# One eight-bank PSUM tile in place of four two-bank tiles, and another hand-written order, in a fused H3 and MLP block

## The chip, the cores and the metric

The kernel runs on one core of one Trainium2 chip. The metric is the device time of one execution in microseconds (us); less is better. TensorE (PE) multiplies matrices into PSUM, ScalarE (ACT) and VectorE (DVE) read PSUM and work in SBUF, GpSimd (POOL) does small set-up work and issues some DMAs, and SyncE (SP) issues the other DMAs.

## The reference

For a sequence of 2048 rows of 640 channels (`q`, in bfloat16) the block computes

```python
xn = layernorm(q)                                  # no scale, no shift
k_shift = sum_t pad(k)[:, t:t+S] * shift_k[:, 3-t] # 4 taps
kv = k_shift * v
y  = irfft(rfft(pad(kv)) * rfft(pad(ssm_k)))[:S]   # causal convolution, length 2048, per channel
s  = xn * (y + kv * ssm_D)
h  = gelu(xn @ w1 + b1)                            # 640 -> 1728, tanh form
g  = silu(h @ w2 + b2)                             # 1728 -> 640
out = q + s * g
```

Two independent paths meet only in the last line: the convolution (K for the filter, U for `kv`) and the two-layer MLP.

## The kernel before, in words

The 2048 rows are 16 tiles of 128 partitions by 640 channels. The convolution is a Fourier transform done in matrix products with two exchanges through scratch memory in HBM. In stage 1 (`stage1`), TensorE multiplies each of the 16 tiles of the filter (tokens `K1_i`) and of `kv` (`U1_i`) with a table `W`; ScalarE or VectorE evicts the pair of PSUM banks to a staging buffer (`Ke_i`, `Ue_i`). The last 128 channels of four tiles go together (`K1r_Q`, `Ker_Q`, `U1r_Q`, `Uer_Q`). Each group Q of four tiles is written to scratch by one DMA of 1280 KB (`Ks_Q`, `Us_Q`); the staging buffer `st` has room for two groups, so a group's first eviction waits until the group two before it has landed. In stage 2, eight slices s are loaded back (`KL_s`, `UL_s`), transformed (`K2`, `U2`, `X2`; evictions `Kf`, `Uf`), multiplied on VectorE (`pr`, `pq`) and transformed back (`i1`, `i1r`; evictions `ie`, `ir`). The results go to scratch (`cs_s`), come back (`cl_r`), and a last product (`i2_i`) gives the convolution, which VectorE multiplies with xn (`ym_i`).

`kv` itself is VectorE's: for each of five groups r of rows (four tiles each in 0 to 2, two each in 3 and 4) a chain of eight steps, `kvr_0`, `kvr_1m`, `kvr_1a` to `kvr_3a`, `kvr_4` (L502 to L511). They read `k` (loads `kl`), the taps (`skl`) and, in the last step, `v` (`vl`).

The MLP works on chunks c of four tiles. `bn_i`, `rs`, `xn_i` make the layer norm; `xt_i`/`xe_i` (TensorE and an eviction) or a transposing DMA (`xT_c`, chunks 2 and 3) turn it. The first layer is `f1_c_r_ft`: five matmuls (L423) into one PSUM bank for 128 of the 1728 hidden channels and 512 rows (256 for the first five of chunk 0), and a gelu on ScalarE (`ge`, L427) that reads the bank. `f1h`/`geh` do the last 64 channels. With `/N` a group is issued as two halves of 64 columns each. The second layer is `f2_i_h`: 14 matmuls (L463) for a tile and half of the channels, a silu (`si_i`, L470), the product with xn (`gx_i`, L473), and at the end the sum with x (`ad_i`) and the store (`os_i`).

Nothing decides at run time or by rule. `plan.op` lists every operation with its engine, what it reads and writes, and which pooled buffers it takes; the string `ORDER` names all operations in the order in which they are recorded, so it is the program order of every engine and of every DMA queue. In a token such as `K1_15@2.0`, the numbers after @ are the places of the buffers that it takes first, here PSUM banks 2 and 3 and staging place 0; `/A`, `/D`, `/G`, `/S` choose ACT, DVE, POOL or SP. The PSUM pool `ps` has eight places, one for each bank of 2 KB in a partition. An operation takes a pair (an even place and the next) or one bank. `emit` (L78) checks that a place is free when it is taken, and sets no semaphore. Those come from the layer below, which follows reads and writes of each declared tile and makes an instruction wait for earlier ones on other engines. In this kernel the eight banks are four tiles of two banks; a pair is a whole tile, and a single is one half of it:

```python
ps_t = [psum.tile([P, 2, 512], F32, name="ps%d" % i)[:] for i in range(4)]        # L155
ps = Pool(8, lambda k, sz: ps_t[k // 2] if sz == 2 else ps_t[k // 2][:, k % 2, :]) # L177
```

Every eviction of `evict` (L175) is one instruction, whatever it evicts; the profile tells them apart by tile (`st`, `k`, `v`, `lat`, `xnT`, `G`). The engines work through their instructions in order, so an instruction that waits holds all behind it.

## Time and profile before

| | |
|---|---|
| median of 3 runs | 226.44 us (223.7 to 226.59) |
| the profiled execution's time | 223.6 us |
| its span (first to last instruction) | 221.8 us |
| TensorE busy | 179.5 us, 81% |
| VectorE busy | 154.7 us, 70% |
| ScalarE busy | 137.9 us, 62% |
| GpSimd busy | 26.5 us, 12% |
| moved by DMA | 51.98 MB, 234 GB/s over the span |
| granted TensorE clock, mean | 0.985 |
| Ks_0 issued, landed | 74.46, 79.89 us |
| Us_3 issued, landed | 100.66, 106.18 us |
| last inverse transform (i1_5) ended | 178.47 us |

The profile is of one execution. Times of instructions are from the start of its span. A line of the list of waits says which engine and line waited for which, for how long in all, how often, and the longest. A line of a timeline gives start, length, engine, source line, operation, what it writes and reads, and in brackets the idle time ahead of it and what ended it. In the chain that ended last, pieces stand in order of time (start, length, what). A token's time is found by counting an engine's instructions in the order of `ORDER`.

### The profile page before, as it was taken

What the parts mean: (1) busy time and instruction counts of PE and PEld (TensorE: products, weight loads), DVE (VectorE), ACT (ScalarE), POOL (GpSimd) and SP (SyncE); (2) the same over time, 40 slices, a digit from 0 to 9 for tenths busy, and PEclk for the clock granted to TensorE, in tenths of its full rate; (3) what the DMA queues carried; (4) which work ended last, traced back from release to release, by engine and by line L of the source; (5) the groups of instructions that cost most, each with busy time, mean ns of one, the idle gap of its engine ahead of it and who ended that gap; (6) DMA issues with size and microseconds to landing.
All of it is one profiled execution on the core that took longest, in us unless ns stands there. A gap on an engine that the chain in (4) does not pass through costs nothing.

```text
span 221.8 us, 5581 instructions
## 1 busy us (share of the span) xinstructions
PE 179.5 (81%) x2405; PEld 105.2 (47%) x2406; DVE 154.7 (70%) x241; ACT 137.9 (62%) x192; POOL 26.5 (12%) x59
## 2 busy tenths in 40 slices
PE   7965795655868998869778978978997799996893
PEld 2434443333323565536455434534443366685792
DVE  7986999999993004669578686877885621786852
ACT  6986696648274986469775868879697672111011
POOL 4831030000000041001500010200200103000000
PEclk9999999999788999999999999999999999999999
DMA  7999957579550499977989942880643356992154
GB/s 202 384 427 417 409 205 259 218 249 415 223 236 3 177 314 336 404 308 240 296 296 192 168 123 92 226 280 5 205 156 118 121 202 206 415 342 114 42 200 148
DMA packets 22299, 51.98 MB, mean 234 GB/s; under 512 B 6657, under 2 KB 15746, under 8 KB 20866
## 3 DMA queue, kind: packets, MB, share of 16 engines
q1 hardware_dynamic: 19968, 41.78, 53.8%
q0 software_dynamic: 2160, 9.83, 12.8%
q8 instruction: 19, 0.31, 0.6%
q14 instruction: 6, 0.05, 0.1%
q10 hardware_dynamic: 146, 0.00, 0.0%
HBM read 31.95 MB, written 18.35 MB: 227 GB/s over the span
## 4 chain that ended last, share of the span: by engine, by line
PE 40%; ACT 27%; DMA 24%; issue 5%; DVE 3%; SPq 1%; ACTq 0%; DVEq 0%
PE ps L423 21%; PE ps L463 10%; ACT st L175 10%; ACT hT L427 8%; DMA scrU<-st 7%; DMA v<-scrC 5%; DMA lat<-scrU 4%; DMA xnT<-xn 4%; PE ps L587 3%; ACT k L175 2%; DMA xn<-in_ssm_k 2%; ACT v L175 2%; DMA scrC<-k 2%; PE ps L544 1%; ACT sl L470 1%
## 5 line engine op out<-in xcount | busy, mean ns | idle before, releaser
L423 PE MATMUL ps<-xnT,w 128*128 128x512 bf16 (+2 forms) x340 | 65.6, 374 | 23.0 <-ACT hT L427 16.6
L463 PE MATMUL ps<-w,hT 128*128 128x320 bf16 (+2 forms) x602 | 64.5, 299 | 3.7 <-ACT st L175 1.3
L463 PEld LDWEIGHTS <-hT 128*128 128x128 bf16 (+2 forms) x602 | 47.4, 104 | 19.4 <-issue 7.1
L423 PEld LDWEIGHTS <-w 128*128 128x128 bf16 (+1 forms) x340 | 29.2, 103 | 54.7 <-issue 36.1
L427 ACT ACTIVATE hT<-ps,b1f 128x512 bf16<-128x512 f32 (+1 forms) x57 | 36.3, 656 | 27.0 <-PE ps L423 26.6
L175 ACT CAST st<-ps 128x1024 bf16<-128x1024 f32 x39 | 37.6, 1021 | 8.4 <-PE ps L338 4.3
L470 ACT ACTIVATE sl<-ps 128x640 bf16<-128x640 f32 (+1 forms) x17 | 11.5, 677 | 32.2 <-PE ps L463 32.1
L473 DVE TENSOR_TENSOR xn<-xn,sl 128x640 bf16<-128x640 bf16 (+1 forms) x17 | 7.9, 465 | 32.2 <-ACT sl L470 32.2
L175 ACT CAST k<-ps 128x1024 bf16<-128x1024 f32 (+2 forms) x22 | 17.9, 855 | 3.5 <-PE ps L544 1.6
L509 DVE TENSOR_TENSOR lat<-lat 128x2560 bf16<-128x2560 bf16 (+1 forms) x15 | 19.4, 1296 | 0.5
L506 DVE TENSOR_TENSOR lat<-k,lat 128x2560 bf16<-128x2560 bf16 (+1 forms) x15 | 18.3, 1222 | 0.3
L175 ACT CAST v<-ps 128x1024 bf16<-128x1024 f32 (+2 forms) x18 | 14.4, 830 | 3.7 <-PE ps L587 1.8
L647 DVE TENSOR_TENSOR xn<-ps,xn 128x640 bf16<-128x640 f32 x16 | 12.7, 818 | 3.7 <-PE ps L643 3.7
L175 DVE CAST k<-ps 128x1024 bf16<-128x1024 f32 (+2 forms) x11 | 9.4, 858 | 8.0 <-PE ps L544 3.6
L370 DVE BATCH_NORM_STATS2 stats<-x 128x6 f32<-128x320 bf16 x32 | 13.6, 468 | 0.2 <-DMA x<-in_x 0.2
L175 DVE CAST lat<-ps 128x1024 bf16<-128x1024 f32 (+2 forms) x9 | 9.1, 1013 | 6.5 <-PE ps L544 2.2
L175 DVE CAST v<-ps 128x1024 bf16<-128x1024 f32 (+2 forms) x8 | 7.6, 955 | 4.6 <-PE ps L587 2.1
L175 ACT CAST lat<-ps 128x1024 bf16<-128x1024 f32 (+2 forms) x12 | 8.2, 728 | 2.6 <-PE ps L544 1.3
L544 PEld LDWEIGHTS <-F 64*32 64x32 bf16 x512 | 5.8, 91 | 8.0 <-issue 4.0
L321 PE MATMUL ps<-hT 128*128 128x512 bf16 x23 | 7.8, 489 | 1.3 <-DVE hT L206 1.2
L587 PE MATMUL ps<-st,I 32*64 32x512 bf16 x256 | 8.3, 379 | 0.0
L528 POOL DMA_DIRECT2D k<-scrK x3 | 2.6, 853 | 47.3 <-DMA scrK<-st 47.1
(98 smaller groups left out, 178.0 us busy)
## 6 DMA issues: line engine op xcount, KB each, us to landing
scrK<-st SPq DMA_DIRECT2D x4, 1280.0 KB, 5.4
scrU<-st SPq DMA_DIRECT2D x4, 1280.0 KB, 6.4
v<-in_v SPq DMA_DIRECT2D x4, 640.0 KB, 12.6
out<-x SPq DMA_DIRECT2D x15, 160.0 KB, 2.5
w<-in_w SPq DMA_DIRECT2D x2, 1120.0 KB, 9.4
x<-in_x SPq DMA_DIRECT2D x3, 640.0 KB, 6.4
k<-in_k SPq DMA_DIRECT2D x3, 640.0 KB, 8.0
k<-scrK POOLq DMA_DIRECT2D x3, 640.0 KB, 5.5
```

Source lines behind the costliest of these rows:

```text
L175: (nc.scalar.copy if e == "ACT" else nc.vector.tensor_copy)(out=out_, in_=in_)
L370: nc.vector.bn_stats(out=stats[:, i, h, :], in_=x_t[:, i, h * H:(h + 1) * H])
L423: nc.tensor.matmul(out=pb.v[us, 0:b - a], lhsT=w1_t[:, ft, t, us], rhs=xnTb[c].v[:, a // P:b // P, t, :], start=(t == 0), stop=(t == DT - 1))
L427: nc.scalar.activation(out=hTb[c].v[:, ft, a:b], in_=pb.v[:, 0:b - a], func=ACT.Gelu_apprx_tanh, bias=b1_f[:, ft:ft + 1], scale=1.0)
L463: nc.tensor.matmul(out=pb.v[us, h, 0:H], lhsT=hTb[c].v[0:M, ft, q * P + us.start:q * P + us.stop], rhs=w2_t[0:M, ft, hs], start=(ft == 0), ...
L470: op("si_" + nm, "ACT", lambda e, hs=hs, n=n: nc.scalar.activation(out=s_.v[:, hs].rearrange("p (h c) -> p h c", c=H), in_=pb.v[:, n[0]:n[ ...
L473: op("gx_" + nm, "DVE", lambda e, hs=hs: nc.vector.tensor_tensor(out=xn_t[:, i, hs], in0=xn_t[:, i, hs], in1=s_.v[:, hs], op=ALU.mult), re ...
L506: op("kv%d_%dm" % (r, j), "DVE", lambda e, i=i, n=n, j=j, t=t, wb=wb: nc.vector.tensor_tensor(out=t.v[:, 0:n, :], in0=k_t[:, i + 3 - j:i + ...
L509: op("kv%d_%da" % (r, j), "DVE", lambda e, n=n, t=t, a=a: nc.vector.tensor_tensor(out=a.v[:, 0:n, :], in0=a.v[:, 0:n, :], in1=t.v[:, 0:n, ...
L544: nc.tensor.matmul(out=pb.v[32 * j:32 * j + 32, a, ri * wd:(ri + 1) * wd], lhsT=F2_t[64 * a:64 * a + 64, ri, :], rhs=B.v[64 * a:64 * a + 6 ...
L587: nc.tensor.matmul(out=pb[j // 2].v[64 * a:64 * a + 64, j % 2, :], lhsT=I1_t[32 * j:32 * j + 32, m, :], rhs=o[w][32 * j:32 * j + 32, a, r, ...
L647: op("ym_%d" % i, "DVE", lambda e, i=i, pb=pb: nc.vector.tensor_tensor(out=xn_t[:, i, :], in0=pb.v.rearrange("p a b -> p (a b)")[:, 0:D], ...
```

## The change

The eight banks are declared as one tile; pairs and singles are views of it at the same places. All the rest of the code is the same. `ORDER` is another permutation of the same 693 operations, with other places for the buffers and in places another engine for an eviction or a queue for a DMA.

```diff
-    ps_t = [psum.tile([P, 2, 512], F32, name="ps%d" % i)[:] for i in range(4)]
+    ps_t = psum.tile([P, 8, 512], F32, name="ps")[:]
...
-    ps = Pool(8, lambda k, sz: ps_t[k // 2] if sz == 2 else ps_t[k // 2][:, k % 2, :])
+    ps = Pool(8, lambda k, sz: ps_t[:, k:k + 2, :] if sz == 2 else ps_t[:, k, :])
...
 ORDER = """
-zz wu0@0 grid fix Dl sm0 c0 wu2@1 b1l wq2 Kl4 wq1 ws2 K1_15@2.0 K1_13@4 sm1 id wq0 sm2 wu5@6 ws1 xl0 bn0 rs0 xl1 bn1
...
-kv1_0@1 kv1_1a kv1_2m@0 kv1_2a kv1_3m@0 kv1_3a kv1_4 Ks_1 U1_1@0.2 kl2 Ue_1/A K1_9@4 Ke_9/A kv2_0@0 kv2_1m@1 kv2_1a
-f1h_0@2 geh_0 kl3 f1_1_0_5/N@3 f1_0_0_10/N@6 ge_0_0_10 f1_0_0_9/N@7 ge_1_0_5 one1 ge_0_0_9 f1_1_0_2/N@0 ge_1_0_2 Ks_2
-U1r_0@4 Uer_0/A U1_0@2 Ue_0/A U1_2@6 kv2_2m@1 kv2_2a kv2_3m@1 kv2_3a Ue_2/A w2l0 vl2 kv2_4 kv3_1m@1 f1_0_1_0@1
-ge_0_1_0 f1_1_0_11@0 ge_1_0_11 kv3_0@0 kv3_1a f1_1_0_8@4 ge_1_0_8 f1_0_0_8@5 ge_0_0_8 vl3 w2l1 U1_3@2 Ue_3/A K1_3@6.0
-Ke_3/A K1_2@0 Ke_2/A f1_1_0_3@4 ge_1_0_3 Da kv3_2m@1 kv3_2a Us_0 f1_1_0_9@5 ge_1_0_9 f1_0_0_12@2 ge_0_0_12 f1_1_0_4@3
-kv3_3m@1 ge_1_0_4 K1r_0@6 K1_0@0 Ker_0/A Ke_0/A one0 kv3_3a kv3_4 K1_1@4 f1_1_0_10@2 f1_0_0_11@3 Ke_1/A Ks_0 KL2/G@0
-xl4 ge_1_0_10 ge_0_0_11 U1_5@6.2 Ue_5/A U1_6@0 Ue_6/A xl5 f2_7_0@4.0 f2_7_1 si_7 U1_4@2 Ue_4/A kv4_0@1 U1r_1@6
-U1_10@0.0 Ue_10/A f2_2_1@4.1 Uer_1/A f2_2_0 U1_7@2 Ue_7/A U1r_2@0 Uer_2/A si_2 U1_9@6 Ue_9/A kv4_1m@0 kv4_1a gx_2
...
+grid zz wu3@0 fix c0 Kl4 wq2 b1l sm0 Dl wu2@1 ws2 wq1 ws1 one1 K1_12@2.0 xl1 Ke_12/A K1_14@4 Ke_14/A K1_13@6 Ke_13/A
...
+kv2_1a Ke_8/A Ks_2 f1_0_0_5@2 kv2_2m@0 kv2_2a kv2_3m@0 ge_0_0_5 f1_0_0_7@3 ge_0_0_7 U1_2@6.2 U1_3@4 Ue_3/A U1_0@0
...
+U1r_0@0 Uer_0/A U1_1@6 Ue_1/A Us_0 f1_1_0_7@2 ge_1_0_7 ge_0_1_0 f1_1_0_9@3 ge_1_0_9 f1_0_0_10@4 ge_0_0_10 K1_2@0.0 kl3
+kv3_0@0 K1_1@6 K1_3@2 kv3_1m@1 kv3_1a Ke_3/A f1_0_0_9@5 Ke_2/A ge_0_0_9 kv3_2m@1 f1_0_0_11@4 ge_0_0_11 kv3_2a Ke_1/A
+Da f1_0_1_4@2 ge_0_1_4 f1_1_0_11@3 ge_1_0_11 K1r_0@0 Ker_0/A K1_0@4 kv3_3m@1 Ke_0/A U1_4@6.2 Ue_4/A f1_0_1_1@2 kv3_3a
+ge_0_1_1 xl5 f2_7_1@0.0 f2_7_0 si_7 U1_5@4 U1_7@6 Ks_0 U1r_1@2 f2_2_1@0.1 Uer_1/A Ue_7/A xl4 vl3 gx_7 kv3_4 Ue_5/A
+U1_6@2 Ue_6/A Us_1 U1r_2@6.0 f2_2_0 U1_11@4 Uer_2/A kv4_0@1 kv4_1m@0 kv4_1a U1_9@2 Ue_11/A si_2 kv4_2m@0 kv4_2a U1_8@6
+Ue_8/A Ue_9/A f2_5_1@4.0 kv4_3m@0 kv4_3a f2_5_0 U1_12@0.2 kv4_4 si_5 gx_5 U1_13@6 Ue_13/A U1_10@2 KL1@0 KL2@1 Ue_12/A
...
+Uf_0_1/A UL2@8 f2_0_0@4.0 U2_2_1@0 Uf_2_1/A pr_1_0@0 X2_1@2 Kf_1_2/A pr_1_1@1 pr_0_0@2 Uf_1_2/A KL4/G@9 K2_4_0@6
...
+Uf_2_2/D ge_3_0_3 pq_1_0@0 i1_0@0.2 pq_0_0 ie_0_0/A xT2@0 pq_0_1 U2_2_0@6 Uf_2_0/D f1_2_0_10@4.0 ge_2_0_10 f1_2_0_1@5
+ie_0_1/D f1_2_0_7@0 ge_2_0_1 UL3@10 ge_2_0_7 pq_1_1 i1r_0@6.2 ir_1_1/A ir_0_0/A ir_1_0/A ir_0_1/A pr_2_1@1 f1_3_0_9@1
...
```

## The prediction, before the changed kernel ran

> **What bounds the kernel now.** I read the page first, then the list of waits, then the timelines of TensorE and ScalarE around the longest waits, then the chain that ended last. "Before TensorE's matmul" below means the idle time ahead of it. The page:

> ```profile
> PE 179.5 (81%) x2405; PEld 105.2 (47%) x2406; DVE 154.7 (70%) x241; ACT 137.9 (62%) x192; POOL 26.5 (12%) x59
> PE   7965795655868998869778978978997799996893
> PEclk9999999999788999999999999999999999999999
> ```

> TensorE is the busiest engine, and its busy row dips to 5 and 6 in slices 3 to 11 (about 11 to 66 us), where no other row is idle for long. From slice 12 on it is mostly at 8 or 9. So about 42 us of TensorE's span is idle, most of it early. The list of waits says for whom (total, times, longest):

> ```profile
> PE ps L423 <- ACT hT L427: 16.6, 15, 2.4
> ...
> PE ps L423 <- ACT hT L443: 5.5, 3, 2.8
> ```

> 22 of the 42 us are one kind: a first-layer matmul (L423) that waits for a gelu. It doesn't need the gelu's result. It waits for a PSUM bank. Which bank is seen around the longest, the matmul at 45.89 (token f1_1_0_5/N@3, bank 3):

> ```profile
> 42.33 0.74 PE L437 MATMUL ps<-xnT,w 128*64 128x256 bf16 x10
> 45.89 2.35 PE L423 MATMUL ps<-xnT,w 128*64 128x512 bf16 x20 [2.83 <-ACT hT L443]
> ...
> 41.59 0.69 ACT L427 ACTIVATE hT<-ps,b1f 128x512 bf16<-128x512 f32 x1 [1.36 <-PE ps L423]
> 42.18 2.83 ACT L175 CAST st<-ps 128x1024 bf16<-128x1024 f32 x3
> 44.88 0.96 ACT L443 ACTIVATE hT<-ps,b1f 64x256 bf16<-64x256 f32 x2
> ```

> Bank 3 was last read by ge_1_0_1, the gelu at 41.59, free at 42.28. The matmul started at 45.89, when geh_0 (44.88 to 45.84) had read bank 2, the other half of the same two-bank tile. The wait list of the built program says the same: it waits for the tile, not for the bank. With one eight-bank tile and the old order, 77 of TensorE's waits move to an earlier instruction in that list, and a matmul into one bank waits for that bank's own reader only; in the new program I find no wait for a neighbour's bank.

> **Part 1, the tile.** For each of these waits I took from the timelines the start of the matmul, the end of TensorE's work before it, and the end of the reader that it really needs. What would be saved on the spot: 0.7 before xt0, 1.8 before f1_0_0_0, 0.5, 0.6, 0.7, 1.3, 1.3, 0.7, 2.8 (f1_1_0_5), 0.7, 2.4 (f1_1_0_11, at 55.25), 0.7, 2.0 (f1_1_0_9, at 65.06), 0.7: 17.0 us up to 70 us. From 129 to 175 us seven more: 1.1, 0.8, 0.3, 0.7, 0.6, 1.2, 1.2: 5.9 us. Two of the early ones cost twice:

> ```profile
> 54.00:55.00 1.00, 0.00 (x0) 0.82 1.03 420
> 55.00:56.00 1.00, 0.75 (x2) 0.50 1.06 442
> 56.00:57.00 1.00, 1.00 (x4) 0.50 1.01 430
> ```

> (us, TensorE busy, granted clock, DMA share, GB/s.) After the idle 2.40 us before f1_1_0_11 the granted clock falls to 0.50, and again after the 2.08 us before f1_1_0_9. The ten matmuls after them took 3.69 and 3.90 us, where ten at full clock take 2.4: another 2.8 us. After the 2.83 us at 43 us the clock stayed at 1.00, so I count these two drops as gone with their gaps, and nothing more. [...] The trace has the drops right behind the gaps.

> **Part 2, the order.** It holds the same work: single-column or split (/N) first-layer groups both take about 1.2 us, so what moves is only what stands ahead of what. I added the incremental durations of the rows (first-layer group 1.19, second-layer half 1.96, ScalarE eviction of two banks 0.91, gelu 0.69, VectorE's kv steps 1.49 and, for the two half groups, 0.82) up to the store that ends each stage. ScalarE's total stays (132.1), VectorE's falls by 1.1. On POOL, 12% busy, two memsets and the scaling of the inverse table (sx) come earlier and hide; KL1 and KL2 go from POOL to SyncE, ahead of Us_2.

> (a) Up to the last store of the filter's first stage (Ks_0, issued at 74.46). TensorE has 47.9 us of work ahead of it before, 52.4 after: +4.5. Minus 17.0 and 2.8: 74.5 + 4.5 - 19.8 = 59.2. ScalarE has 51.7 us ahead of it, its first eviction starts at 5.7, and its first gelu brings 1.28 us that the sums leave out (in the chain at 16.16): 58.7 in all, so with TensorE at 59.2 it would have to run without a pause. Two in-order queues as full as that hold each other up: I give back 4 us, a fifth of the gain (bounds: 0 and all 19.8), and take 63.

> (b) Up to the landing of the last U store (Us_3, 106.18). The new SyncE order is Us_0, kl3, xl5, Ks_0, xl4, vl3, Us_1: two loads that used to go out by 46.84 now stand behind stores, and what is behind those waits too. kl3 is needed by kv3_0 and goes out with Us_0, which has 38.5 us of TensorE's work ahead of it, so near 48; it lands near 54 (1.9 MB at the rate below), and VectorE ended kv2 at 59.7. vl3 is needed by kv3_4. How fast transfers go in this stage:

> ```profile
> 74.50:80.00 5.50, 5.30 (x46) 3.51 (x45) 0.00 (x0) 5.47 (x7) 0.00 (x0) 1.00 0.87 300
> 80.00:106.20 26.20, 22.85 (x274) 14.59 (x272) 15.29 (x35) 17.71 (x21) 5.08 (x8) 1.00 0.89 322
> ```

> About 318 GB/s (last column). Ks_0, xl4 and vl3 are 2.6 MB, 8.2 us: vl3 lands at 71.2. kv3_4 and the eight steps of kv4, 9 x 0.82: 78.6. Last U matmuls (0.8) and two evictions (1.8): 81.2; a store alone takes 5.5 (Us_3 did): 86.7. But from Ks_0 to Us_3 the queues carry four stores of 1.31 MB (Ks_0, Us_1 to Us_3) and five loads of 0.66 (xl4, vl3, KL0 to KL2), 8.5 MB, 26.8 us at that rate: 89.8, and I take this later one: 16.4 us earlier than before. VectorE isn't in the way: before, kv4 stood behind gx_2 (68.6 to 86.4, idle); now it doesn't. [...] Us_1, with four POOL loads in flight, took 10.64 us and Us_3 5.53; if the queues were independent, the sum would be 202 instead.

> (c) To the last inverse transform (i1_5, ended 178.47) it was 72.3 us:

> ```profile
> 84.86 10.64 DMA scrU<-st
> ...
> 100.66 5.53 DMA scrU<-st
> ...
> 107.23 9.80 DMA lat<-scrU
> ...
> 208.39 9.73 PE ps L463 x140
> ```

> The chain goes from that landing through the U loads and then along TensorE. TensorE's work in it is 66.3 before, 66.6 after. Of the 5.9 us of bank waits I count 4 as gained: 89.8 + 72.3 + 0.3 - 4 = 158.4. UL3 now follows both transposes on SyncE; xT2 landed 9.4 us after issue, and TensorE has about 9 us of work between, so I charge nothing, and 2 us if that cover is gone.

> (d) To the end: 43.3 us before, nearly all TensorE; 0.7 us of its work now stands ahead of i1_5 instead. The last core stores (cs) and their reload took 10.4 us from i1_5 to i2_4, covered by 9.8 us of second-layer work; in the new order 11.1 us stand there. 158.4 + 42.6 = 201.0.

> The profiled execution had a span of 221.8 and a time of 223.6, 1.8 outside. 202.8 on that scale; the median of the runs (226.44) is 1.3% above that execution, so 205.5 as a time to be measured.

> **Rivals.** *Half comes back* (25%). ScalarE becomes the wait. For it: 58.7 against 59.2 in (a). Against it: ScalarE's gelus waited 26.6 us for L423 in the old order, so it was itself held by the bank waits. Half of 25.7: 223.6 - 12.9 = 210.7, as a median 213. *No change* (9%). The U path is set by VectorE's kv chain (9.8 of 10 us busy from 30 to 60) and by transfers, and TensorE's idle time only moves. Against: VectorE sat idle 17.8 us at 68.6, waiting for a silu behind TensorE. 224 to 228. *Slower: the stores hold ScalarE* (9%). Uer_2 now waits for Ks_0's landing (staging slot 0), Ue_13 for Us_1's, and behind each, gelus and evictions queue in order, and TensorE behind those when its banks are full. TensorE has 8 to 10 us of work between the last filter matmul and Uer_2; if the packed stores take Us_1's 10.64 instead of 5.4, it stalls. If ScalarE has also eaten all 19.8 of (a), Ks_0 goes at 79.0 and lands at 89.6, Us_1 near 100; from Us_1's landing to Us_3's it was 10.7 (95.5 to 106.2), so Us_3 lands at 111, 4.5 us later than before: 228, as a median 231. It decides once Ks_0 is issued after about 74. *The declaration doesn't free the banks*, or ties all eight: 1%; the wait lists speak against it; then 240 and more.

> **How the numbers follow.** The forecast (56%) is 197 to 210: 197 is without the 4 us of (a), the 2 of (c) and most of (b)'s transfer bound (3.1), 210 gives back 4.5 more. The half-back case reaches to 219. Faster by over 2% (about what a measurement of this kernel can tell from no change) is below 221.9: 56 + 25, 0.81; within 2% 0.09; slower 0.10. The range 197 to 220 leaves out the last three cases.

> **What would show it.** Right: the two waits of L423 for L427 and L443 together under 8 us; PEclk without dips after slice 2; Ks_0 issued at 60 to 66, Us_3 landed at 87 to 93, span 196 to 208. Wrong: ScalarE evictions waiting for scrK or scrU for over 5 us, kv3_4 idle for vl3 past 75 us, or TensorE's waits for hT unchanged.

## The result and the profile after

The changed kernel takes 192.05 us (median, 191.75 to 192.54) against 226.51 for the kernel before in the same comparison (223.7 to 227.97): a ratio of 0.852, with a 95% interval of 0.844 to 0.860. Here and below, a median is of all runs of a kernel, a ratio of those within 1.5% of its fastest. The forecast was 205.5, its range 197 to 220: the direction was right, the time lies below the range, and the gain was 34.5 us where 20.9 had been forecast. The profiled execution took 192.54 us, with a span of 190.8.

The page of the kernel after: busy time and instructions of each engine, then TensorE's busy tenths and the granted clock in 40 slices (4.8 us each).

```profile
PE 176.1 (92%) x2377; PEld 103.8 (54%) x2377; DVE 153.9 (81%) x241; ACT 138.7 (73%) x194; POOL 30.0 (16%) x61
PE   7889999999889874999979999999999999999991
PEclk9999999999999996699999999999999999999998
```

TensorE has the same products to make, and 14.7 us of idle time in place of 42. The dips to 5 and 6 in slices 3 to 12 are gone. One dip is new, in slices 15 and 16, and behind it the clock falls to half (0.50): from 73 to 80 us. The list of TensorE's waits says what stands there, and what no longer stands there:

```profile
PE ps L544 <- DMA k<-scrK: 3.6, 1, 3.6
PE ps L463 <- ACT st L175: 1.3, 2, 0.7
...
PE ps L544 <- DMA lat<-scrU: 0.8, 1, 0.8
```

The two lines of 16.6 and 5.5 us, L423 waiting for a gelu, have no counterpart. The longest wait is for a load. The chain that ended last follows it (start, length, what):

```profile
61.55 12.34 DMA k<-scrK
...
73.94 1.05 PE ps L544 x27
74.99 3.85 PE ps L463 x14
...
81.81 5.50 DMA scrU<-st
...
88.42 11.57 DMA lat<-scrU
```

From the issue of KL1 at 61.55 the chain goes through the load, K2_1_0 and K2_1_1 (L544), a second-layer half at half clock (14 matmuls in 3.85 us, which take 2.01 elsewhere) and the last U store to the U loads. Between 20 and 66 us three engines are nearly full at once, as one stretch of the windows of this kernel shows (busy us of PE, PEld, DVE, ACT, POOL, then clock, DMA share, GB/s):

```profile
20.00:66.00 46.00, 43.44 (x331) 23.20 (x330) 44.80 (x37) 43.76 (x63) 5.47 (x4) 1.00 0.99 375
```

Where the 31.0 us of span went, by three anchors: when Us_3 landed, when i1_5 ended, the end of the span; and TensorE's idle time in the two later stretches (length less busy time in the windows between the anchors). The other rows are the experiments below.

| kernel | Ks_0 issued | Us_3 landed | from there to i1_5 (TensorE idle) | from i1_5 to the end (idle) | span |
|---|---|---|---|---|---|
| before | 74.5 | 106.2 | 72.3 (10.8) | 43.3 (7.2) | 221.8 |
| after | 52.9 | 87.3 | 64.4 (1.7) | 39.1 (4.3) | 190.8 |
| tile_alone | 54.4 | 88.2 | 69.8 (8.1) | 42.7 (6.6) | 200.7 |
| order_alone | 73.9 | 105.9 | 77.9 (12.1) | 39.1 (4.3) | 222.9 |
| k2_late | 53.8 | 82.6 | 65.8 | 39.1 | 187.5 |
| new_tail | 55.2 | 90.4 | 69.6 | 39.7 | 199.7 |
| old_head | 57.1 | 90.8 | 64.9 (2.0) | 38.9 (4.4) | 194.5 |
| new_head | 52.9 | 86.0 | 66.8 (3.1) | 43.8 (7.7) | 196.6 |
| gap_filled | 52.4 | 83.2 | 64.7 | 38.6 | 186.6 |

So 18.9 us were gained before Us_3 landed, 7.9 between that and i1_5, 4.2 behind it.

### The profile page after: what moved, and what is told of

Its sections match the earlier page's. It is cut to its first block, busy times and chain, and to the rows that moved or that the text cites. A ratio compares the mean times of both kernels' runs of the same rounds, so it can differ in the third digit from the quotient of the medians.

```text
span 190.8 us, 5537 instructions
## 1 busy us (share of the span) xinstructions
PE 176.1 (92%) x2377; PEld 103.8 (54%) x2377; DVE 153.9 (81%) x241; ACT 138.7 (73%) x194; POOL 30.0 (16%) x61
## 4 chain that ended last, share of the span: by engine, by line
PE 44%; DVE 31%; DMA 20%; issue 2%; ACT 1%; SPq 1%; POOL 0%; POOLq 0%; DVEq 0%
PE ps L423 15%; PE ps L463 15%; DVE lat L506 8%; DVE lat L509 8%; DMA k<-scrK 6%; DMA lat<-scrU 6%; PE ps L587 4%; DMA lat<-scrC 4%; DVE stats L370 3%; PE ps L544 3%; DMA scrU<-st 3%; DVE lat L502 3%; DVE v L511 2%; PE ps L643 2%; DVE xn L391 1%
## 5 line engine op out<-in xcount | busy, mean ns | idle before, releaser
L463 PE MATMUL ps<-w,hT 128*128 128x320 bf16 (+2 forms) x588 | 66.8, 303 | 3.3 <-ACT st L175 1.3
L423 PE MATMUL ps<-xnT,w 128*128 128x512 bf16 (+3 forms) x325 | 61.0, 362 | 0.0
L463 PEld LDWEIGHTS <-hT 128*128 128x128 bf16 (+2 forms) x588 | 48.0, 105 | 20.2 <-issue 6.9
L423 PEld LDWEIGHTS <-w 128*128 128x128 bf16 (+1 forms) x325 | 26.8, 101 | 28.4 <-issue 4.8
L175 ACT CAST st<-ps 128x1024 bf16<-128x1024 f32 x39 | 38.2, 1041 | 2.4 <-DMA scrU<-st 1.2
L427 ACT ACTIVATE hT<-ps,b1f 128x512 bf16<-128x512 f32 (+1 forms) x57 | 35.2, 679 | 3.7 <-PE ps L423 3.4
L470 ACT ACTIVATE sl<-ps 128x640 bf16<-128x640 f32 (+1 forms) x17 | 11.5, 675 | 31.8 <-PE ps L463 30.3
L175 ACT CAST k<-ps 128x1024 bf16<-128x1024 f32 (+2 forms) x25 | 18.8, 775 | 4.3 <-PE ps L544 3.7
L175 DVE CAST k<-ps 128x1024 bf16<-128x1024 f32 (+2 forms) x12 | 12.1, 1022 | 10.1 <-ACT hT L427 2.4
L506 DVE TENSOR_TENSOR lat<-k,lat 128x2560 bf16<-128x2560 bf16 (+1 forms) x15 | 19.4, 1294 | 0.3
L175 ACT CAST v<-ps 128x1024 bf16<-128x1024 f32 (+2 forms) x20 | 16.7, 858 | 2.1 <-PE ps L615 1.2
L647 DVE TENSOR_TENSOR xn<-ps,xn 128x640 bf16<-128x640 f32 x16 | 12.8, 817 | 2.4 <-PE ps L643 2.4
L544 PEld LDWEIGHTS <-F 64*32 64x32 bf16 x512 | 6.0, 92 | 8.9 <-DMA k<-scrK 3.9
L175 DVE CAST lat<-ps 128x1024 bf16<-128x1024 f32 (+2 forms) x9 | 8.2, 921 | 1.5 <-PE ps L587 0.9
L544 PE MATMUL ps<-k,F 64*32 64x256 bf16 x224 | 5.1, 291 | 3.6 <-DMA k<-scrK 3.6
L175 ACT CAST lat<-ps 128x1024 bf16<-128x1024 f32 (+2 forms) x8 | 6.3, 804 | 1.9 <-PE ps L544 1.6
L511 DVE TENSOR_TENSOR v<-lat,v 128x2560 bf16<-128x2560 bf16 (+1 forms) x5 | 6.1, 1225 | 0.5 <-DMA v<-in_v 0.4
## 6 DMA issues: line engine op xcount, KB each, us to landing
k<-in_k SPq DMA_DIRECT2D x3, 640.0 KB, 11.1
```

Of the source, the lines that this page charges most:

```text
L175: (nc.scalar.copy if e == "ACT" else nc.vector.tensor_copy)(out=out_, in_=in_)
L423: nc.tensor.matmul(out=pb.v[us, 0:b - a], lhsT=w1_t[:, ft, t, us], rhs=xnTb[c].v[:, a // P:b // P, t, :], start=(t == 0), stop=(t == DT - 1))
L427: nc.scalar.activation(out=hTb[c].v[:, ft, a:b], in_=pb.v[:, 0:b - a], func=ACT.Gelu_apprx_tanh, bias=b1_f[:, ft:ft + 1], scale=1.0)
L463: nc.tensor.matmul(out=pb.v[us, h, 0:H], lhsT=hTb[c].v[0:M, ft, q * P + us.start:q * P + us.stop], rhs=w2_t[0:M, ft, hs], start=(ft == 0), ...
L470: op("si_" + nm, "ACT", lambda e, hs=hs, n=n: nc.scalar.activation(out=s_.v[:, hs].rearrange("p (h c) -> p h c", c=H), in_=pb.v[:, n[0]:n[ ...
L506: op("kv%d_%dm" % (r, j), "DVE", lambda e, i=i, n=n, j=j, t=t, wb=wb: nc.vector.tensor_tensor(out=t.v[:, 0:n, :], in0=k_t[:, i + 3 - j:i + ...
```

## The experiments

### The tile alone, the order alone (tile_alone, order_alone)

The first has the old order with the new declaration, the second the new order with the old one.

```diff
 tile_alone, against the kernel before (ORDER unchanged)
-    ps_t = [psum.tile([P, 2, 512], F32, name="ps%d" % i)[:] for i in range(4)]
+    ps_t = psum.tile([P, 8, 512], F32, name="ps")[:]
-    ps = Pool(8, lambda k, sz: ps_t[k // 2] if sz == 2 else ps_t[k // 2][:, k % 2, :])
+    ps = Pool(8, lambda k, sz: ps_t[:, k:k + 2, :] if sz == 2 else ps_t[:, k, :])
```

> The old order with the one eight-bank tile. If the waits for a neighbour's bank were in TensorE's way, most of the 22.9 us of waits and 2.8 us of half clock that the trace of before shows come back: 201 to 208 us, no L423 wait for a gelu over 1 us, no granted clock of 0.50 at 55 and 65 us. If instead the new order is what counts and the waits were slack, 218 to 227 us.

Measured: 203.57 us, ratio to before 0.903 (0.892 to 0.914). The bank waits count: 22 us by the ratio, 23.5 by the medians, where 25.7 had been added up on the spot. In the list of TensorE's waits no L423 waits for a gelu any more, and loads stand at its head:

```profile
PE ps L544 <- DMA lat<-scrU: 3.1, 1, 3.1
PE ps L559 <- DMA k<-scrU: 2.2, 1, 2.2
```

> The new order with the four two-bank tiles. Laid on the trace of after, 30 of TensorE's operations would start before the reader of the neighbour's bank is done, 37.9 us in all. If the waits count, 212 to 230 us, so possibly no faster than before. If the order does the work by itself, 192 to 200 us.

Measured: 224.25 us, ratio 0.992 (0.987 to 0.998). The order without the tile is worth almost nothing (about 2 us), because the waits for the neighbour's bank come with it again. The list of waits of order_alone:

```profile
PE ps L423 <- ACT hT L427: 18.5, 18, 2.1
...
PE ps L423 <- DVE xnT L175: 2.9, 2, 1.8
PE ps L423 <- ACT hT L443: 2.8, 2, 1.8
```

Its Us_3 lands at 105.9, as before, and its middle stretch is the longest in the table: 77.9 us, 13.5 more than with the same order and one tile. Only its tail is already as short as after the change. By the ratios the tile gives 22 us to the old order and 32 to the new one; the order gives 2 us by itself and 11.5 on top of the tile.

### Two tiles of four banks (two_tiles_of_four)

If a matmul waits for the whole declared tile, larger tiles should cost more, until the tile is all eight banks.

```diff
-    ps_t = [psum.tile([P, 2, 512], F32, name="ps%d" % i)[:] for i in range(4)]
+    ps_t = [psum.tile([P, 4, 512], F32, name="ps%d" % i)[:] for i in range(2)]
-    ps = Pool(8, lambda k, sz: ps_t[k // 2] if sz == 2 else ps_t[k // 2][:, k % 2, :])
+    ps = Pool(8, lambda k, sz: ps_t[k // 4][:, k % 4:k % 4 + 2, :] if sz == 2 else ps_t[k // 4][:, k % 4, :])
```

> The old order with two tiles of four banks. If a wait is for the whole tile wherever the tile is not all of PSUM, each wait now covers four banks: laid on the trace of before, 81 TensorE operations would start too early by 93 us in all, so 260 to 310 us. If the number of tiles makes no difference as long as a tile has more than two banks, it is like the one tile, 201 to 208 us.

Measured: 320.31 us in its one run, a little over what was expected, with a span of 318.5. Beside L423's wait for gelus, the list of its waits has kinds that the kernel before doesn't have, pairs that wait for other pairs:

```profile
PE ps L423 <- ACT hT L427: 12.8, 16, 1.4
PE ps L338 <- ACT st L175: 6.1, 8, 1.7
...
PE ps L643 <- DVE xn L647: 5.4, 4, 2.2
```

TensorE is busy for 212.2 us instead of 179.5 (half clock: its mean clock is 0.878) and idle for 106.3 instead of 42.3. The two differences, 32.7 and 64.0, are the 96.7 us by which the span grew. In order of tile size the same program order takes 227 (two banks), 320 (four) and 204 (eight). That is no smooth dependence. It fits a tile of two or four banks that is waited for as a whole, and a tile of all eight that is waited for bank by bank. Why the layer below treats that one otherwise, no run here tells.

### The new wait taken away (k2_late)

K2_1_0 stands ahead of the last U tiles (U1_15, U1r_3, U1_14) in the new order, and waits for KL1. Here the two products and their evictions go behind Us_3.

```diff
-... f2_6_1@4.0 K2_1_0@6 Ue_10/A Kf_1_0/A K2_1_1@0 Kf_1_1/A f2_6_0 Us_2 ... Ue_14/A Us_3 f2_4_0
+... f2_6_1@4.0 Ue_10/A f2_6_0 Us_2 ... Ue_14/A Us_3 K2_1_0@6 Kf_1_0/A K2_1_1@0 Kf_1_1/A f2_4_0
```

> After with K2_1_0 and K2_1_1, which waited 3.6 us for the load KL1 and were followed by 6 us at half clock, moved behind the last U matmul and its evictions. If that wait delays the last U store, Us_3 is issued at 75 to 77 us instead of 81.8, the half clock at 74 to 80 us is gone, and the time falls to 186 to 190. If the transfers set the landing of Us_3 anyway (8.5 MB from Ks_0 on), Us_3 lands at 86 to 88 as in after and the time stays at 191 to 193.

Measured: 188.87 us, ratio to before 0.835 (0.821 to 0.849); the profiled execution is 3.2 us shorter than that of after. Us_3 is issued at 75.9 instead of 81.8, 3.4 us after VectorE's last kv step. Of the 4.7 us by which it lands earlier 1.5 are lost in the middle stretch, where K2_1 now has to be done and a load is waited for (1.43 us, again followed by a stretch at a clock of 0.50, from 93.0 to 96.4 us).

### Is it the gap that halves the clock? (gap_filled)

The load is waited for as before, but TensorE is kept busy meanwhile.

```diff
+    fb = Buf(pool=ps)
+
+    def fill(e):
+        for _ in range(13):
+            nc.tensor.matmul(out=fb.v, lhsT=hT_t[1][:, 0, 0:P], rhs=hT_t[1][:, 0, :], start=True, stop=True)
+
+    op("fill", "PE", fill, writes=[fb])
...
-... f2_6_1@4.0 K2_1_0@6 ...
+... f2_6_1@4.0 fill@6 K2_1_0@6 ...
```

> The changed kernel with 13 more matmuls (128x128 by 128x512, into a bank that nothing reads afterwards) between f2_6_1 and K2_1_0, in the 3.58 us in which TensorE waits for KL1. The output is unchanged. They take 2.8 to 3.2 us at full clock, so the load is waited for as before and K2_1_0 starts at about 73.9; only the idle gap shrinks to under 1 us. Theory: the half clock after it comes from the gap; then f2_6_0 takes 2.1 to 2.4 us instead of 3.92, the U matmuls behind it 0.3 to 0.5 less, and the time falls by 1.5 to 2.2 us to 190 to 190.6. Rival: the clock falls for another reason (load on the chip at that time), f2_6_0 stays at 3.9 and the time at 192 or above. Second rival: the clock drop is off the path, since Us_3 waits for ScalarE's evictions: f2_6_0 becomes short and the time stays at 192.

Measured: 189.95 us, ratio 0.831 (0.826 to 0.836). TensorE around the place, first after, then gap_filled (start, length, engine, line, operation; L463 and L544 of the one are L471 and L552 of the other):

```profile
73.94 1.05 PE L544 MATMUL ps<-k,F 64*32 64x256 bf16 x32 [3.58 <-DMA k<-scrK]
74.92 3.92 PE L463 MATMUL ps<-w,hT 128*128 128x320 bf16 x14
```

```profile
68.96 2.97 PE L329 MATMUL ps<-hT 128*128 128x512 bf16 x13
72.47 0.63 PE L552 MATMUL ps<-k,F 64*32 64x256 bf16 x32 [0.54 <-DMA k<-scrK]
73.03 2.08 PE L471 MATMUL ps<-w,hT 128*128 128x320 bf16 x14
```

With 13 matmuls of no use in the gap, K2_1 takes 0.63 us instead of 1.05 and f2_6_0 2.08 instead of 3.92. The theory holds: with an idle time of 0.54 us instead of 3.58 the granted clock is 1.00 here, where it was 0.50 in the kernel after (73.1 to 79.9 us). And the half clock was on the path, since the loads and stores around it stand in the same order. From the start of K2_1_0 to the issue of Us_3 it is 5.22 us instead of 7.87, which is 2.65 for the clock, more than the 1.5 to 2.2 expected. The span is 4.2 us shorter; the other 1.5 us come from a KL1 that was issued 1.0 us sooner and landed 1.5 us sooner. That lies ahead of the edit, so I don't put them down to it.

### Which part of the order brings what (new_tail, old_head, new_head)

All three have the eight-bank tile and join the two orders at one point: the operations up to it in the one order, all that is left in the other, with a few buffer places changed where the joint needs it.

```diff
 new_tail: the old order up to i1_5 and its evictions, then the new one
 old_head: the old order up to Us_3, then the new one
 new_head: the new order up to Us_3, then the old one
```

> One eight-bank tile; the old order up to the last inverse transform and its evictions, then the rest in the new order. With the tile and the old order alone it was 203.6 us, with the new order 192.05. Theory: the order's 11.5 us lie where the two traces differ, 5.5 between the landing of Us_3 and i1_5, 3.6 behind i1_5, 0.9 ahead of Us_3; so this one gets the 3.6 alone: i1_5 still ends near 158, the stretch behind it takes 39 instead of 42.7, about 200 us. Rival: the tail is short in the new order because of what the earlier parts leave to it (loads and products already made), then it is still 42 to 43 and the time 203 to 204.

Measured: 200.14 us (196.4 to 201.5; before in the same comparison 227.9). The runs lie too far apart for a ratio: three took 200.1 to 201.5 with a mean clock of 0.974 to 0.981, and one, without a profile, 196.4 with 0.997. So the time by itself proves little. In the profiled execution, one of the three, the stretch behind i1_5 takes 39.7 us instead of the 42.7 of tile_alone: 3.0 of the 3.6, with the old order's middle ahead of it. The rival, 42 to 43, falls.

> One eight-bank tile; the old order up to the issue of Us_3, then the rest in the new order. Theory: ahead of Us_3 the order is worth under 1 us, so Us_3 lands near 88, and from there the new order takes its 64 and 39 us: 192 to 194 us. Rival: the new order's early part sets up the later one (KL1 and KL2 loaded early, two K2 transforms already made, other buffer places), and without it the later part loses half of its gain: 196 to 199 us.

Measured: 195.02 us (191.9 to 196.3), between the two expectations, ratio 0.849 (0.841 to 0.857), the same as the changed kernel's 0.852 within the intervals. So the new order's early part is worth no more than the 2 us or so that can be told apart here, if the later part is new. The profiled execution lies above the median, at 196.27, with Us_3 landed 3.5 us later than in the changed kernel and two drops of the clock to 0.50 ahead of that (3.41 us each, from 42.8 and 80.4); its last two stretches, 64.9 and 38.9, are those of the changed kernel.

> One eight-bank tile; the new order up to the issue of Us_3, then the rest in the old order. Theory: the early part is worth under 1 us by itself and the later one brings back the old order's pauses (loads that come late, 7 us; the tail, 3.6): 201 to 204 us, as with the old order throughout. Rival: the early part sets up the later one: 196 to 199 us.

Measured: 198.60 us, ratio 0.874 (0.869 to 0.879). Here my theory (201 to 204) was wrong and the rival right. The tail is the old one again (43.8 us), but the middle stretch takes 66.8 us, not 69.8. The loads that the old order waits for there are waited for less. The timeline of TensorE in tile_alone, then in new_head:

```profile
89.81 0.41 PE L544 MATMUL ps<-v,F 64*32 64x256 bf16 x16 [1.29 <-DMA v<-scrK]
...
99.08 0.63 PE L544 MATMUL ps<-lat,F 64*32 64x256 bf16 x32 [3.09 <-DMA lat<-scrU]
```

```profile
90.71 0.41 PE L544 MATMUL ps<-v,F 64*32 64x256 bf16 x16 [0.94 <-DMA v<-scrK]
...
97.82 0.63 PE L544 MATMUL ps<-lat,F 64*32 64x256 bf16 x32 [0.93 <-DMA lat<-scrU]
```

The waits of the middle stretch can thus be shortened from either side, by the early part of the new order or by the later one, and the two gains don't add. Which of the early part's moves does it (KL1 and KL2 sooner, two K2 products already made, U stored 2 us sooner) wasn't taken apart.

## Why the prediction was right in direction and too small

**Part 1, the tile, was right in mechanism and nearly in size.** The waits for the neighbour's bank are gone. By tile_alone, 25.7 us on the spot were 22 in the time. In part (a) I took 19.8 us off the issue of Ks_0; tile_alone issues it at 54.4, 20.1 us earlier. The two drops of the clock went with their gaps, as I had said from the rows: tile_alone's clock is 1.00 up to 128.4 us.

**Part 2 (a), Ks_0 at 63: measured 52.87.** Three things were wrong. First, "+4.5": I counted all of TensorE's work that stands ahead of Ks_0 in the order. Ks_0 waits only for the evictions of its own four tiles. Up to the last matmul of these, TensorE is busy for 45.8 us in tile_alone and for 47.6 in the kernel after: +1.8. A store's place in the order says nothing of the matmuls of others in front of it. order_alone shows the new order at no cost here (73.9 against 74.5). Second, no run shows the 4 us given back for "two in-order queues as full as that": the window from 20 to 66 shows TensorE 94%, VectorE 97% and ScalarE 95% busy at once. They did run almost without a pause. These two are 6.7 of the 10.1 us. Third, I kept the pauses that the tile leaves in the old order: ahead of those matmuls TensorE is idle for 5.6 us in tile_alone and for 2.9 in the kernel after. ScalarE's 58.7 had the first error too: in the kernel after, from its first eviction (6.05) to its last one for Ks_0 (52.84) it is busy for 46.2 us and idle for 0.6. So it is ScalarE that sets the issue of Ks_0 now, with no pause left, but 5.9 us sooner than I had it.

**(b), Us_3 landed at 89.8: measured 87.31, by two errors that nearly cancel.** Ks_0 was issued 10.1 us sooner than I had it, and from there to the landing of Us_3 it took 34.4 us where I had 26.8. That the sum came near is luck. VectorE's part went as worked out: kv3_4 began at 63.48, right behind the landing of vl3 (63.39), and nine steps of 0.82 make 70.9, where kv4 did end. From there I had 2.6 us to the issue of Us_3; k2_late has 3.4. The changed kernel has 10.9, since K2_1_0 stands in between and waits 3.58 us for KL1, and then the half clock comes (0.50, 73.1 to 79.9 us). I had costed KL1 only as 0.66 MB among the transfers, not as a wait ahead of U1_15. The price of the transfers themselves was about right: in k2_late, which lacks this wait, it took 28.8 us from the issue of Ks_0 to the landing of Us_3, with a DMA share of 1.00 all along. In the kernel after they ran nearly dry for a while:

```profile
60.10:81.80 21.70, 17.41 (x139) 10.06 (x140) 13.72 (x21) 13.34 (x16) 1.81 (x2) 0.84 0.75 270
```

This is the stretch from the landing of Ks_0 to the issue of Us_3 in the kernel after: a DMA share of 0.75, 270 GB/s, a clock of 0.84. The mean hides two parts: up to 75.5 us the share is 1.00 (356 GB/s), and from there to 81.8, until Us_3 can go, 0.14 (60 GB/s). Without the new wait, Us_3 would have landed 7.2 us before my forecast (k2_late: 82.6).

KL1, 0.66 MB, was in flight for 12.34 us beside Us_1 and KL2 from SyncE and KL0 and KL3 from POOL, and in these 12.34 us the DMA share was 1.01, at 348 GB/s. It is the one of these loads that TensorE waited for, for 3.58 us.

**(c), 68.6 us to i1_5: measured 64.4.** I credited 4 us and let the rest of TensorE's idle time stay. The idle time fell from 10.8 to 1.7. With the tile alone it was still 8.1: the bank waits went, and waits for loads took their place, because TensorE now came to the loads sooner. The new order removes these: old_head, with the old order up to Us_3, has 64.9. Which of the later part's moves does it was not taken apart.

**(d), 42.6 us to the end: measured 39.1.** I moved 0.7 us of work and kept the pauses of the old tail. The timeline of TensorE before:

```profile
201.40 0.46 PE L643 MATMUL ps<-v,G 128*64 128x512 bf16 x4 [1.55 <-DMA v<-scrC]
...
208.39 9.72 PE L463 MATMUL ps<-w,hT 128*64 128x320 bf16 x140 [0.92 <-DVE xn L647]
```

i2_12 waited for its load (cl_6, which on SyncE stood behind the store os_3), and f2 for VectorE's ym. In the new tail the longest pause is 0.28 us. Idle time fell by 2.9 us, and 1.35 us of matmuls moved ahead of i1_5. new_tail shows it as a gain of the tail's own.

**The scale.** I went from a span of 201.0 to 205.5: 1.8 outside the span, and 1.3% for the median above the profiled execution. Measured: the median is 0.5 us below the profiled execution, and 1.3 above its span. The 1.3% was the spread of the kernel before, not a property of the profile.

The sum: (b) 2.5, (c) 4.2, (d) 3.5, the scale 3.2 and rounding are the 13.4 us between 205.5 and 192.05. The error of (a) is inside (b), where the new wait hides most of it. The steps that failed are on the order's side: it was costed as work that moves, with the old order's pauses kept unless a bank explained them, and with no pause of its own.

**The signs.** L423's wait for gelus under 8 us: right, none is listed. The clock without dips after slice 2: wrong, the new gap made one. Ks_0 at 60 to 66: wrong, earlier. Us_3 landed at 87 to 93: right, for the wrong reasons. Span 196 to 208: wrong, 190.8. kv3_4 waited 0.41 us for vl3, at 63 us; no eviction waited over 1.2 us for scrU. Of the rivals, that ScalarE becomes the wait came true for Ks_0, as worked out under (a), but not at its price: half of the gain was to be lost, and it was exceeded. The slower case needed Ks_0 after 74. The rival by which VectorE's kv chain sets the U path was right in one thing: in the chain of the kernel after, that chain of steps (L502 to L511) is the path from 19 to 61 us. By this chain VectorE, and not TensorE, sets the U path in this stage now; it hardly pauses there, and the gain came all the same.

## What to carry to other kernels

Look at the reader of the very bank a matmul writes: if it was done long before (here at 42.28, with the matmul at 45.89), the wait is for the declared tile and not for the data, and the added-up waits are a good price for the declaration (25.7 us here, 22 in the time). Cost a new order twice, once with the pauses that the old order has and once without them, since an order that removes the waits for loads can be worth as much as the trace of before shows in idle time of the engine that sets the end (in the middle stretch here, TensorE's idle time fell by 9.1 us and the length by 7.9). Ahead of a store that others wait for, put nothing that waits for a load still in flight: here it cost a wait of 3.58 us and then 2.65 us for the half clock.

## What the runs showed of the hardware

TensorE's idle time in the 3.41 us at full clock ahead of a drop was 1.76 us or more for the 12 drops of before, after, tile_alone, order_alone, k2_late, new_tail and new_head, 1.26 and 1.62 for the two of old_head, and 1.48 or more in two_tiles_of_four. With a trace divided into stretches of 3.41 us, counted both ways from its first drop, the most idle time in a stretch with no drop behind it was 1.79 (1.80 in two_tiles_of_four). The two ranges overlap, so the runs show no limit. For the gaps in the prediction I have an estimate from these figures only: three times 3.41 us ahead of the first drop of the kernel before (54.66) is 44.4, and that divides the gap of 2.83 us (43.07 to 45.89), which no drop follows, into 1.35 and 1.47, while the gap of 2.08 us (62.98 to 65.06), which brought one, has 1.9 in one stretch. No run tests this. What a drop costs is an estimate as well: half of 3.41 us, 1.7 us of TensorE's work. Measured, without the 6.83 us at half clock of the kernel after, gap_filled took 2.65 us less from K2_1_0 to the issue of Us_3.

The kernel after, us by us (TensorE busy, clock, DMA share, GB/s), with the clock still 1.00 in the gap and 0.50 behind it:

```profile
72.00:73.00 1.00, 0.00 (x0) 1.00 1.06 361
73.00:74.00 1.00, 0.06 (x8) 0.54 1.17 454
74.00:75.00 1.00, 1.00 (x33) 0.50 1.04 434
```

**The same order took 227.1 us with four PSUM tiles of two banks, 320.3 with two of four and 203.6 with one of eight.** In the lists of TensorE's waits L423 waits for a gelu (hT L427) for 16.6 us in the first and 12.8 in the second, and the third has no such line. That the waits went by the declared tile in the first two, and by the bank in the third, is my reading of these figures.
